# Pooling v in two halves of the heads, with three pairs of the first up matmul begun early

## The chip, the cores and the metric

The kernel runs on one core of a Trainium2 chip. The metric is the device time of one execution in microseconds (us); the time of a kernel is the median over its runs. The engines are called as in the profile: PE is TensorE (PEld its weight loads), DVE is VectorE, ACT is ScalarE, POOL is GpSimd, SP is SyncE. PSUM, into which PE writes, has eight banks of 512 fp32 values per partition. The kernel uses all of them: three pairs, called `banks[0]` to `banks[2]`, and two single ones, `obanks[0]` and `obanks[1]`.

## The reference

Attention over keys and values that are pooled by 8 along the sequence, and then a layer with the gate h * cos(h). Sizes: 8 batches, 8 heads, 576 positions, 64 values per head; the layer goes from 512 to 2048 and back, over 8 x 576 = 4608 tokens.

```python
def _attn_ref(q, k, v) -> np.ndarray:
    B, H, S, D = q.shape
    pool = 8
    Sp = S // pool
    scale = 1.0 / np.sqrt(D)
    k_p = k.reshape(B, H, Sp, pool, D).mean(axis=3)
    v_p = v.reshape(B, H, Sp, pool, D).mean(axis=3)
    scores = scale * np.matmul(q, k_p.transpose(0, 1, 3, 2))
    scores = scores - np.max(scores, axis=-1, keepdims=True)
    attn = np.exp(scores)
    attn = attn / (np.sum(attn, axis=-1, keepdims=True) + 1e-09)
    return np.matmul(attn, v_p).astype(np.float32)

def _moe_ref(x, w_in, w_out) -> np.ndarray:
    h = x @ w_in
    g = h * np.cos(h)
    return (g @ w_out).astype(np.float32)
```

Between the two, the attention's output is laid out as `x` with one row per token and 512 columns, head by head.

## The kernel before

The work runs over nine token tiles of 512 (`NT`, loop at L561). For tile t the kernel does an **up** stage (x times `w_in`, the gate) and a **down** stage (times `w_out`), and between these matmuls it puts the attention of batch t + 1, whose output fills the next tiles' x. x is held transposed in one SBUF tile, `xT`: 128 partitions by four chunks (`KCH`) by 4608 tokens. A chunk holds two heads, so chunks 0 and 1 are heads 0 to 3, and chunks 2 and 3 are heads 4 to 7.

The program's order on each engine is the order in which the code is written (`manual_schedule`, L53); what an instruction must wait for on other engines follows from the tiles that it reads and writes. So an instruction that waits holds up all that stands behind it on its engine.

Before tile 0, batch 0's attention runs alone (L533 to L556). Its first 512 positions are cut into four units, `BY_HEADS` (L50): units 0 and 1 are the positions 0 to 255 and 256 to 511 of heads 0 to 3, units 2 and 3 the same of heads 4 to 7. For each unit:

- `scores` (L222) multiplies pooled keys and transposed queries, and ACT takes the exponential (L240);
- `sums_first` (L306) sums the exponentials over the 72 pooled positions with a block of ones (four matmuls, L312), and ACT makes the inverse by a logarithm and an exponential (L316, L317);
- `values_then` (L320) multiplies the exponentials by the pooled values (four matmuls, L326), and DVE multiplies by the inverse and writes the unit's part of `xT` (L328).

`pool_v_mm` (L181) pools v: for each of 9 rows and each half of the partitions one matmul with the matrix `groups` (18 in all, L185), all heads at once, into both banks of a pair; then DVE copies the sums to `vz` (L187), from which `values_then` takes its weights. v is the last of batch 0's loads. While it travels, warm-up matmuls (L527), the pooling of k (L177), the transposes of q (L214), the scores and the first two units' sums run.

The tail of that stage is the part that the change touches. In order on PE: pooling of v into `banks[1]`; sums of unit 2 into `obanks[0]`; values of unit 0 into `obanks[1]`; values of unit 1 into `banks[1]`; sums of unit 3 into `banks[2]`; values of unit 2 into `obanks[1]`; values of unit 3 into `obanks[0]`. Then the first up matmuls begin.

An up stage has eight pairs of 128 hidden columns (`fp`, in tile 0 in the order 0 to 7). `up_mm` (L347) sums a pair's product over the four chunks into one pair of banks: four matmuls for chunks 0 and 1, four for chunks 2 and 3 (L353). In tile 0 the pairs take `banks[0]`, `banks[1]` and `banks[2]` in turn (L344). `up_g` (L357) takes the cosine on ACT (L363), for which the sine's table must be loaded (`sin_tables`, L333), and then the product on DVE (L367), which frees the banks for the third pair after. In tile 0 the chunks 0 and 1 of pairs 0 and 1 are multiplied before the loop (L557, L558), since they need only heads 0 to 3; the loop then does their chunks 2 and 3 (L568), and all four chunks of the later pairs. The weights `w_in` come in four blocks (`load_w_in`, L510 and L514), one for two pairs each.

Loads that change fp32 to bf16 are issued by POOL in the order of the code: for batch 0 q, k, q, v, then three blocks of `w_in`, then k and q of batch 1, the last block of `w_in`, and so on (L487 to L522).

Of the kernel before, what the change touches and what calls it, by code (L numbers as in the profile page):

```python
# [20 lines left out]
def kernel(  # L21
# [9 lines left out]
    nc = tc.nc  # L31
    B, H, S, D = q.shape
    Sp = S // POOL
# [4 lines left out]
    KCH = d_model // 128  # L38
# [45 lines left out]
    banks = [psum.tile([128, 2, 512], FP32, name=f"bank{i}") for i in range(3)]  # L84
    obanks = [psum.tile([128, 512], FP32, name=f"obank{i}") for i in range(2)]
# [51 lines left out]
    def v_part(b):  # L137
        return vz[b % 2][:, :, 0:4:3, :]
# [31 lines left out]
    def pool_k_mm(b, bank, pj0, pj1):  # L170

        kb = staged["k", b]
        ps = bank[:, 0:(pj1 - pj0) * Sp].rearrange("p (j n) -> p j n", n=Sp)
        for pj in range(pj0, pj1):
            for t in range(ROW):
                for rows in half:
                    nc.tensor.matmul(ps[rows, pj - pj0, :], lhsT=kb[rows, pj, t, :], rhs=groups[rows, t, :],  # L177
                                     start=(t == 0), stop=(t == ROW - 1))
        return lambda copy: put_kk(b, ps, pj0, pj1, copy)

    def pool_v_mm(b, pair):  # L181
        vb = staged["v", b]
        for t in range(ROW):
            for hp, rows in enumerate(half):
                nc.tensor.matmul(pair[:Sp, hp, 0:KCH * D], lhsT=groups[rows, t, :], rhs=vb[rows, :, t, :],  # L185
                                 start=(t == 0), stop=(t == ROW - 1))
        nc.vector.tensor_copy(out=v_part(b).rearrange("p j a d -> p a j d"),  # L187
                              in_=pair[:Sp, :, 0:KCH * D].rearrange("p a (j d) -> p a j d", j=KCH))

    def k_transpose(b):  # L190
        for i in range(2):
            nc.sync.dma_start_transpose(out=kk[b % 2][:, i * H // 2:(i + 1) * H // 2],
                                        in_=ring[b % 2][:, i:i + H].rearrange("p h d -> p (h d)"))
# [10 lines left out]
    def q_transpose(b):  # L204
        qT_tile(b)
        nc.sync.dma_start_transpose(out=att["qT", b], in_=q_flat(b))

    def q_transpose_mm(b, bank, g0, g1):

        if ("qT", b) not in att:  # L210
            qT_tile(b)
        ps = bank.bitcast(BF16)[:, 0:(g1 - g0) * 128].rearrange("p (g n) -> p g n", n=128)
        for g in range(g0, g1):
            nc.tensor.matmul(ps[:, g - g0, :], q_flat(b)[:, g * 128:(g + 1) * 128], identity, is_transpose=True)  # L214
        return lambda copy: copy(out=att["qT", b][:, g0:g1, :], in_=ps)

    def ex_col(u, i):

        (c0, n), (h0, nh) = u
        return (i // 2 % 2 * (nh // 2) + i // 4 * 2 + i % 2) * n  # L220

    def scores(b, u, pair):  # L222
        scores_mm(b, u, pair)
        scores_exp(b, u, pair)
# [19 lines left out]
    def x_out(b, u, rows):  # L244
        (c0, n), (h0, nh) = u
        return xT[rows, h0 // 2:(h0 + nh) // 2, b * S + c0:b * S + c0 + n]

    def cols(x, u):
        n = u[0][1]
        return x[:, 0:n * u[1][1] // 2].rearrange("p (j n) -> p j n", n=n)  # L250
# [3 lines left out]
    def inverse_tile(w):  # L254

        if early_inverses:
            name = early_inverses.pop(0)
            return msb.tile([128, 2, 256], FP32, name=name, tag=name, bufs=1).rearrange("p a m -> p (a m)")[:, 0:w]
        inv = asb.tile([128, 512], FP32, name="inv", tag="inv", bufs=1)
        return inv[:, 0:w]  # L260
# [45 lines left out]
    def sums_first(b, u, cs):  # L306

        (c0, n), (h0, nh) = u
        ex = att["ex", b, u]
        for i in range(nh):  # L310
            hp = i % 2
            nc.tensor.matmul(cs[hp * 64:hp * 64 + 64, (i // 2) * n:(i // 2 + 1) * n], lhsT=ones[:Sp, :],  # L312
                             rhs=ex[:, ex_col(u, i):ex_col(u, i) + n])
        w = nh * n // 2
        inv = inverse_tile(w)
        nc.scalar.activation(out=inv, in_=cs[:, 0:w], func=ACTF.Ln)  # L316
        nc.scalar.activation(out=inv, in_=inv, func=ACTF.Exp, scale=-1.0)  # L317
        att["inv", b, u] = inv

    def values_then(b, u, ao):  # L320

        (c0, n), (h0, nh) = u
        ex = att.pop(("ex", b, u))
        for i in range(nh):
            pj, hp = divmod(h0 + i, 2)
            nc.tensor.matmul(ao[hp * 64:hp * 64 + 64, (i // 2) * n:(i // 2 + 1) * n],  # L326
                             lhsT=vz[b % 2][:, pj, 3 * hp, :], rhs=ex[:, ex_col(u, i):ex_col(u, i) + n])
        nc.vector.tensor_mul(out=x_out(b, u, slice(0, 128)), in0=cols(ao, u), in1=cols(att.pop(("inv", b, u)), u))  # L328
# [4 lines left out]
    def sin_tables():  # L333
        nc.scalar.preload_act_table_set("trig_and_small")


    def up_order(t):
        n = FFCH // 2
        return range(n) if t < FIRST else [i + a * n // 2 for i in range(n // 2) for a in range(2)]

    def up_bank(t, fp):
        i = list(up_order(t)).index(fp)
        if t < FIRST:
            return banks[i % 3]  # L344
        return (banks[0], banks[2], banks[1], obanks)[i % 4 if i < 7 else 0]

    def up_mm(t, fp, k0=0, k1=KCH):  # L347

        h = up_bank(t, fp)
        for j in range(2):  # L350
            fc = 2 * fp + j
            for ki in range(k0, k1):
                nc.tensor.matmul(h[j] if h is obanks else h[:, j, :], lhsT=w_in_sb[fc // 4][:, ki, (fc % 4) * 128:(fc % 4 + 1) * 128],  # L353
                                 rhs=xT[:, ki, t * TILE:(t + 1) * TILE],
                                 start=(ki == 0), stop=(ki == KCH - 1))

    def up_g(t, fp, between=()):  # L357
        h = up_bank(t, fp)
        cos = msb.tile([128, 2, TILE], FP32, name="cos", tag="cos", bufs=2)
        g = g_sb[:, 2 * fp:2 * fp + 2, :]  # L360
        parts = [(h[j], cos[:, j], g[:, j]) for j in range(2)] if h is obanks else [(h, cos, g)]
        for ps, c, _ in parts:
            nc.scalar.activation(out=c, in_=ps, func=ACTF.Sin, bias=half_pi[:, :1])  # L363
        for put, copy in between:
            put(copy)
        for ps, c, o in parts:
            nc.vector.tensor_mul(out=o, in0=ps, in1=c)  # L367
# [31 lines left out]
    def put_gs(*kis):  # L399
        for k, i in kis:  # L400
            put_g(k, i)
# [93 lines left out]
    groups = g3.rearrange("p f n -> p (f n)")[:, 0:ROW * Sp].rearrange("p (t n) -> p t n", t=ROW)  # L495
# [34 lines left out]
    us = BY_HEADS  # L530
# [16 lines left out]
    warm_up(2, banks[1][:, 0, :])  # L547
    scores(0, us[2], banks[0])
    scores(0, us[3], banks[2])
    pool_v_mm(0, banks[1])  # L550
    sums_first(0, us[2], obanks[0])
    values_then(0, us[0], obanks[1])
    values_then(0, us[1], banks[1][:, 0, :])
    sums_first(0, us[3], banks[2][:, 0, :])
    values_then(0, us[2], obanks[1])
    values_then(0, us[3], obanks[0])  # L556
    up_mm(0, 0, 0, 2)  # L557
    up_mm(0, 1, 0, 2)  # L558
    sin_tables()

    for t in range(NT):  # L561
        b = t + 1
# [2 lines left out]
            for fp in up_order(t)[0:2]:  # L565
                up_mm(t, fp, 0, 2)
        for n, fp in enumerate(up_order(t)):
            up_mm(t, fp, 2 if n < 2 else 0)  # L568
            between = ()
            if t == 0:  # L570
                if fp == 4:
                    puts = pool_k_mm(1, obanks[0], 0, 2), pool_k_mm(1, obanks[1], 2, 4)
                elif fp in (5, 6):
                    g0 = 9 * (fp - 5)
                    puts = q_transpose_mm(1, obanks[0], g0, g0 + 5), q_transpose_mm(1, obanks[1], g0 + 5, g0 + 9)
                if fp in (4, 5, 6):
                    puts[0](vec)
                    between = ((puts[1], act),)
            up_g(t, fp, between)
            if 0 < t and 3 <= n < 6:  # L580
                put_gs(*[(k, 0) for k in (((3,), (1,), ()) if t == 1 else ((1, 2), (3,), (4,)))[n - 3]])
            if 0 < t and b < B:
                if n == 0:
                    q_transpose(b)
                    k_transpose(b)
                elif n == 2:
                    pool_rest(b, "v")
                    if b + 1 < B:
                        nc.gpsimd.tensor_copy(out=gate, in_=kk[b % 2][0:1, H - 1, 0:1])
                        load_q(b + 1)  # L590
                        load_kv(b + 1, "v", v)
            if n == 2:
                while stores:
                    stores.pop(0)()
# [155 lines left out]
```

The softmax here doesn't subtract the row's maximum and nothing guards it: scores larger than these inputs give would overflow.

## Time and profile before

| | |
|---|---|
| time, median of 4 runs | 286.49 us (286.07 to 287.55) |
| the profiled execution, its own time | 287.55 us |
| its span, first to last instruction | 285.8 us |
| granted PE clock, mean | 1.00 |
| stretch 13.16 to 18.34 us: PE, DVE, ACT busy | 3.58, 2.02, 4.49 us of 5.18 |
| stretch 18.34 to 36.50 us: PE, DVE, ACT busy | 18.16, 12.55, 13.38 us of 18.16 |
| DMA in both stretches | 206 and 207 GB/s |

The stretches are cut where the work changes: from 13.16 the last scores of batch 0 and the tail just described, from 18.34 the up stage of tile 0 with the pooling of batch 1's k and the transposes of its q between. Times in the trace count from the first instruction. An engine's busy time is what its rows add up to; a matmul's row lasts from its start until its last result is written, so that rows of matmuls that follow each other overlap, and the pace is read from their starts. An idle time is put down to the semaphore that ended it.

### The profile page before, as it was taken

The page shows a single profiled execution, that of the slowest core. Times are in us where ns is not written, and L with a number is a line of the kernel's source. Part 1 is how long each engine was busy: PE and PEld are TensorE (multiplying, and loading weights), DVE is VectorE, ACT ScalarE, POOL GpSimd, SP SyncE. Part 2 cuts the span into 40 slices and gives each one's busy share as a digit, 9 for nine tenths or more (in the row PEclk, how much of TensorE's full clock was granted, in tenths as well). Part 3 has the DMA queues.
Part 4 walks back from the last instruction along what each step waited for, and adds up shares of the span by engine and source line. Part 5 has one row for each costly group of instructions (what it writes and reads, how often), then busy time and mean ns, then how long its engine had stood idle before and what let it go on. Part 6 is the DMA issues. An engine that isn't in the chain of part 4 may idle for free.

```text
span 285.8 us, 5857 instructions
## 1 busy us (share of the span) xinstructions
PE 277.0 (97%) x2360; PEld 176.8 (62%) x2360; DVE 215.3 (75%) x314; ACT 164.4 (58%) x193; POOL 143.0 (50%) x150
## 2 busy tenths in 40 slices
PE   7889999999999999999999999999999999999994
PEld 3445554445874597458845884588448844874583
DVE  5547747899966995699569956995699569856972
ACT  3677798377356745665566556565556555436600
POOL 8453159997499349934993399439900000000000
PEclk9999999999999999999999999999999999999999
DMA  7999999592929798998677968892670252005014
GB/s 148 200 205 206 207 205 214 104 213 37 166 40 150 128 226 137 144 145 182 101 141 144 183 94 159 137 189 55 115 158 3 55 117 50 0 20 129 2 37 110
DMA packets 57738, 36.12 MB, mean 126 GB/s; under 512 B 35441, under 2 KB 53361, under 8 KB 57713
## 3 DMA queue, kind: packets, MB, share of 16 engines
q0 software_dynamic: 19744, 18.07, 41.3%
q1 hardware_dynamic: 37328, 17.18, 29.3%
q10 hardware_dynamic: 640, 0.52, 0.8%
q8 instruction: 18, 0.29, 0.4%
q14 instruction: 8, 0.06, 0.1%
HBM read 36.70 MB, written 9.44 MB: 161 GB/s over the span
## 4 chain that ended last, share of the span: by engine, by line
PE 86%; DVE 6%; ACT 3%; DMA 2%; issue 1%; POOL 0%; DVEq 0%; POOLq 0%; ACTq 0%
PE bank L353 35%; PE obank L431 32%; PE obank L370 4%; PE obank L353 4%; PE bank L233 3%; DVE g_sb L367 3%; DMA q_b<-in_q_dram 2%; PE bank L295 2%; PE bank L431 2%; PE bank L268 1%; DVE w L387 1%; DVE g L397 1%; ACT cos L363 1%; ACT ex L240 1%; DVE vz L187 0%
## 5 line engine op out<-in xcount | busy, mean ns | idle before, releaser
L353 PE MATMUL bank<-xT,w_in_sb 128*128 128x512 bf16 x512 | 114.0, 379 | 0.2 <-DVE g_sb L367 0.2
L363 ACT ACTIVATE cos<-bank,half_pi 128x1024 f32<-128x1024 f32 x64 | 70.3, 1113 | 57.0 <-PE bank L353 55.1
L353 PEld LDWEIGHTS <-w_in_sb 128*128 128x128 bf16 x576 | 56.1, 98 | 66.3 <-issue 0.9
L367 DVE TENSOR_TENSOR g_sb<-bank,cos 128x1024 bf16<-128x1024 f32 x64 | 77.1, 1218 | 25.1 <-ACT cos L363 24.8
L156 POOL TENSOR_TENSOR half_sums<-kv_st 72x512 f32<-72x512 bf16 x48 | 54.8, 1168 | 0.6 <-issue 0.2
L240 ACT ACTIVATE ex<-bank 72x1024 bf16<-72x1024 f32 (+1 forms) x40 | 35.0, 928 | 34.0 <-PE bank L233 33.8
L431 PEld LDWEIGHTS <-g 128*128 128x128 bf16 x512 | 47.9, 98 | 6.1 <-issue 0.3
L431 PE MATMUL obank<-w,g 128*128 128x256 bf16 x368 | 42.7, 272 | 0.2 <-DVE p_sb L445 0.2
L431 PEld LDWEIGHTS <-g_sb 128*128 128x128 bf16 x384 | 36.7, 98 | 6.9 <-DVE g_sb L367 0.3
L162 POOL TENSOR_TENSOR half_sums<-half_sums 72x512 f32<-72x512 f32 x24 | 30.4, 1289 | 0.0
L431 PE MATMUL obank<-w_out_sb,g_sb 128*128 128x256 bf16 x240 | 28.9, 273 | 0.0
L397 DVE TENSOR_TENSOR g<-g_sb 128x1024 bf16<-128x1024 bf16 x32 | 23.3, 729 | 0.5
L714 POOL COPY gate<-g 1x1 bf16<-1x1 bf16 x5 | 0.9, 180 | 34.5 <-DVE g L397 34.5
L279 DVE TENSOR_TENSOR xT<-bank,inv 64x256 bf16<-64x256 f32 x14 | 5.9, 422 | 15.0 <-ACT inv L275 14.9
L300 DVE TENSOR_TENSOR x_rows<-bank,inv_rows 128x512 bf16<-128x512 f32 x24 | 16.6, 691 | 0.8
L431 PE MATMUL obank<-w_out_sb,g 128*128 128x256 bf16 x112 | 15.6, 273 | 0.0
L431 PE MATMUL obank<-w,g_sb 128*128 128x256 bf16 x128 | 15.3, 273 | 0.0
L370 PE MATMUL obank<-w_out_sb,g_sb 128*128 128x512 bf16 x64 | 15.2, 379 | 0.0
L353 PE MATMUL obank<-xT,w_in_sb 128*128 128x512 bf16 x64 | 15.1, 379 | 0.0
L233 PE MATMUL bank<-qT,kk 64*72 64x128 bf16 (+2 forms) x288 | 12.7, 221 | 0.1
L233 PEld LDWEIGHTS <-kk 64*72 64x72 bf16 x288 | 8.8, 110 | 5.3 <-issue 3.8
L331 ACT ACT_TABLE_LOAD x9 | 11.5, 1283 | 0.9 <-PEq L734 0.8
(103 smaller groups left out, 277.6 us busy)
## 6 DMA issues: line engine op xcount, KB each, us to landing
out_dram<-o_two SPq DMA_DIRECT2D x64, 128.0 KB, 2.4
kv_st<-in_v_dram POOLq DMA_DIRECT2D x8, 576.0 KB, 11.4
kv_st<-in_k_dram POOLq DMA_DIRECT2D x7, 576.0 KB, 8.2
q_b<-in_q_dram POOLq DMA_DIRECT2D x6, 576.0 KB, 7.5
w_in_sb<-in_moe_w_in_dram POOLq DMA_DIRECT2D x4, 512.0 KB, 14.5
w_out_sb<-in_moe_w_out_dram POOLq DMA_DIRECT2D x4, 512.0 KB, 18.2
q_b<-in_q_dram POOLq DMA_DIRECT2D x4, 288.0 KB, 13.2
g_sb<-in_k_dram SPq DMA_DIRECT2D x1, 576.0 KB, 3.5
```

The source lines that it names most:

```text
L156: nc.gpsimd.tensor_tensor(out=s[:, h:h + 2], in0=x[:, h:h + 2, 0:4, :], in1=x[:, h:h + 2, 4:8, :], op=ADD)
L162: add(out=s[:, h:h + 4, 0:2, :], in0=s[:, h:h + 4, 0:2, :], in1=s[:, h:h + 4, 2:4, :], op=ADD)
L233: nc.tensor.matmul(pair[:Sp, bank, c:c + n].rearrange("p (g n) -> p g n", n=64), lhsT=kk[b % 2][half[r], key_slot(b, h0 + i, r), 0:Sp], rh ...
L240: nc.scalar.activation(out=ex[:, 0:nh * n].rearrange("p (a n) -> p a n", a=2), in_=pair[:Sp, :, 0:nh * n // 2], func=ACTF.Exp, scale=scale ...
L300: nc.vector.tensor_tensor(out=x[0:n].rearrange("p (j a d) -> p j a d", j=KCH, a=2), in0=ps[0:n, :, 0:2 * (D + 2)].rearrange("p j (a w) -> ...
L331: nc.scalar.preload_act_table_set("natural_log_exp_and_others")
L353: nc.tensor.matmul(h[j] if h is obanks else h[:, j, :], lhsT=w_in_sb[fc // 4][:, ki, (fc % 4) * 128:(fc % 4 + 1) * 128], rhs=xT[:, ki, t * ...
L363: nc.scalar.activation(out=c, in_=ps, func=ACTF.Sin, bias=half_pi[:, :1])
L367: nc.vector.tensor_mul(out=o, in0=ps, in1=c)
L370: nc.tensor.matmul(o, lhsT=g_sb[:, fc, ms * 128:(ms + 1) * 128], rhs=w_out_sb[fc // 4][:, fc % 4, :], start=(fc == 0), stop=(fc == FFCH - 1))
L397: nc.vector.tensor_tensor(out=out[:, f0:f1], in0=x, in1=y, op=op)
L431: mms.append(lambda bank=bank, first=first, g=g, w=w, fc=fc, p=p: nc.tensor.matmul(bank[p], lhsT=g(fc, p), rhs=w(fc), start=(first and fc ...
```

## The change

`pool_v_mm` takes a range of chunks, and pools and copies these alone; without a range it does all four, as it does for batch 1. For batch 0 it is called twice: chunks 0 and 1 (heads 0 to 3), and chunks 2 and 3 after the values of unit 0. The 18 matmuls on 256 columns become twice 18 on 128 columns, the copy of 512 values per partition becomes two of 256. Both halves write to the first columns of `banks[1]`.

The order of the tail becomes: first half of v; values of unit 0 (`obanks[1]`); second half of v; values of unit 1 (now `obanks[0]`); sums of unit 2 (now `banks[0]`); values of unit 2 (`obanks[1]`); sums of unit 3 (`banks[2]`); values of unit 3 (`obanks[0]`). Chunks 0 and 1 of three pairs, not two, are then multiplied before the loop, and the loop leaves them out for three pairs in tile 0.

```diff
-    def pool_v_mm(b, pair):
+    def pool_v_mm(b, pair, j0=0, j1=KCH):
         vb = staged["v", b]
         for t in range(ROW):
             for hp, rows in enumerate(half):
-                nc.tensor.matmul(pair[:Sp, hp, 0:KCH * D], lhsT=groups[rows, t, :], rhs=vb[rows, :, t, :],
+                nc.tensor.matmul(pair[:Sp, hp, 0:(j1 - j0) * D], lhsT=groups[rows, t, :], rhs=vb[rows, j0:j1, t, :],
                                  start=(t == 0), stop=(t == ROW - 1))
-        nc.vector.tensor_copy(out=v_part(b).rearrange("p j a d -> p a j d"),
-                              in_=pair[:Sp, :, 0:KCH * D].rearrange("p a (j d) -> p a j d", j=KCH))
+        nc.vector.tensor_copy(out=v_part(b)[:, j0:j1].rearrange("p j a d -> p a j d"),
+                              in_=pair[:Sp, :, 0:(j1 - j0) * D].rearrange("p a (j d) -> p a j d", d=D))
...
     scores(0, us[3], banks[2])
-    pool_v_mm(0, banks[1])
-    sums_first(0, us[2], obanks[0])
+    pool_v_mm(0, banks[1], 0, 2)
     values_then(0, us[0], obanks[1])
-    values_then(0, us[1], banks[1][:, 0, :])
+    pool_v_mm(0, banks[1], 2, 4)
+    values_then(0, us[1], obanks[0])
+    sums_first(0, us[2], banks[0][:, 0, :])
+    values_then(0, us[2], obanks[1])
     sums_first(0, us[3], banks[2][:, 0, :])
-    values_then(0, us[2], obanks[1])
     values_then(0, us[3], obanks[0])
-    up_mm(0, 0, 0, 2)
-    up_mm(0, 1, 0, 2)
+    for fp in range(3):
+        up_mm(0, fp, 0, 2)
     sin_tables()
...
         for n, fp in enumerate(up_order(t)):
-            up_mm(t, fp, 2 if n < 2 else 0)
+            up_mm(t, fp, 2 if n < (3 if t == 0 else 2) else 0)
```

## The prediction

> **What bounds the kernel now.** I read the page's busy times first, then the chain that ended last, in order of time, then the timeline of the stretch that the change touches.
>
> ```profile
> span 285.8 us, 5857 instructions
> PE 277.0 (97%) x2360; PEld 176.8 (62%) x2360; DVE 215.3 (75%) x314; ACT 164.4 (58%) x193; POOL 143.0 (50%) x150
> ...
> 15.74 0.70 DVE vz L187
> ...
> 18.37 8.80 PE bank L353 x40
> 27.17 1.29 PE obank L177 x72
> 28.46 1.83 PE bank L353 x8
> ```
>
> TensorE is the bound. It is idle 8.8 us in all; the table by stretch puts 1.6 us of that into 13.16 to 18.34, the tail of batch 0's attention, and none into 18.34 to 36.5. From 18.34 the chain is TensorE without a break, so what moves the first up matmul, or opens a gap in the up stage, is paid in full. Now the timeline (start, duration, engine, line, count, idle before and its releaser):
>
> ```profile
> 14.47 1.17 PE L185 MATMUL bank<-kv_st,g 64*72 64x256 bf16 x18 [0.69 <-DMA kv_st<-in_v_dram]
> 15.57 0.41 PE L312 MATMUL obank<-ex,ones 72*64 72x256 bf16 x4
> 15.74 0.69 DVE L187 CAST vz<-bank 72x512 bf16<-72x512 f32 x1 [2.66 <-ACT ex L240]
> 16.03 0.60 ACT L316 ACTIVATE q_sb<-obank 128x512 f32<-128x512 f32 x1
> 16.48 0.41 PE L326 MATMUL obank<-ex,vz 72*64 72x256 bf16 x4 [0.50 <-DVE vz L187]
> 16.72 0.39 PE L326 MATMUL bank<-ex,vz 72*64 72x256 bf16 x4
> 16.94 0.39 PE L312 MATMUL bank<-ex,ones 72*64 72x256 bf16 x4
> 17.00 0.69 DVE L328 TENSOR_TENSOR xT<-obank,p_sb 128x512 bf16<-128x512 f32 x1 [0.58 <-PE obank L326]
> 17.75 0.63 PE L326 MATMUL obank<-ex,vz 72*64 72x256 bf16 x8 [0.42 <-DVE xT L328]
> 18.34 8.83 PE L353 MATMUL bank<-xT,w_in_sb 128*128 128x512 bf16 x40
> 19.06 1.28 ACT L334 ACT_TABLE_LOAD   x1
> 21.13 1.11 ACT L363 ACTIVATE cos<-bank,half_pi 128x1024 f32<-128x1024 f32 x1 [0.79 <-PE bank L353]
> 22.28 1.23 DVE L367 TENSOR_TENSOR g_sb<-bank,cos 128x1024 bf16<-128x1024 f32 x1 [2.51 <-ACT cos L363]
> ```
>
> v lands at 14.47, and nothing before that moves. The pooling, its copy and the products follow in turn, with two waits of 0.50 and 0.42.
>
> The rows from 18.34 on decide my forecast. The 40 up matmuls follow each other by (8.83 - 0.38)/39 = 0.217 us. Pair 0 (half of it begun early, then pair 1's half, then its rest) is whole after 12 matmuls, 18.34 + 2.60 = 20.94; its cosine starts 0.19 later and its product ends at 22.28 + 1.23 = 23.51. Pair 3 reuses bank 0 and has its turn after 24 matmuls, at 18.34 + 5.20 = 23.54. **The bank comes free 0.03 us before it is wanted: there is no slack.**
>
> **The change part by part.** Lags, all from these rows: TensorE to VectorE 0.10, TensorE to ScalarE 0.05, VectorE to TensorE 0.05, ScalarE to VectorE 0.04. VectorE rows follow each other 0.08 before the nominal end (17.00, then 17.61), ScalarE's Ln and Exp by 0.63. Four products take 0.41, the next group of the same tile shape starts 0.23 after them, one of another shape 0.07 before their end (15.57 against 15.64).
>
> *Half the pooling.* The 256-column matmuls follow by (1.17 - 0.27)/17 = 0.053 us. The Trainium skill (TensorE: Matmul & The Clock Gate, "Wait — 56ns, not 53.3ns?") gives columns / 2.4 GHz + 2.5 ns one after another: 109 ns for 256 columns, 56 for 128. The row shows half of that, since the two row halves of the array work side by side, so I take 0.027 for 128 columns. By the row a half takes 17 x 0.027 + 0.21 (a 128-column transposing matmul's own time, from L214: five in 0.45 at 0.056) = 0.67; by the rule 1.16. I take the row and keep the other end: L177's 72 matmuls in 1.36, each with its own weights, show that loading does not hold them at 0.05.
>
> *Half the copy.* 256 elements: 0.42 (L279 with 256 elements a partition took 422 ns, L328 with 512 took 691, L187 with 512 took 686). Two halves cost 0.84 for 0.69.
>
> *The switches of shape.* The Trainium skill (TensorEngine Tiling (Array Packing), "Key Properties") says that changing the tiling mode drains TensorE, which speaks against putting the second half between two groups of products: two switches more. The row prices one: the next group starts 0.07 before the last end, so some 0.15 of overlap is lost at each (0.2 after the last issue where 0.05 is usual). By the row that is 0.3 of TensorE's time; with no drain 0. I count it, though waits cover most of it.
>
> In order, then (us of the span):
> - half 1 14.47 to 15.14; copy 1 15.24 to 15.66; values of unit 0 15.71 to 16.12 (before: 16.48, so 0.77 earlier);
> - half 2 16.05 to 16.72; values of unit 1 16.65 to 17.06; sums of unit 2 16.88 to 17.29;
> - VectorE: product of unit 0 16.22 to 16.91, copy 2 16.83 to 17.25, product of unit 1 17.17 to 17.86;
> - values of unit 2 wait for copy 2: 17.30 to 17.71; sums of unit 3 17.53 to 17.94; values of unit 3 need obank 0, which the product of unit 1 reads until 17.86: 17.91 to 18.32. Behind this wait on TensorE stands only the up stage;
> - up begins at 18.28: **0.06 gained of the 0.77**. The wait that is late next is VectorE: copy 2 and the two products fill it from 16.22 to 17.86.
> - ScalarE gets the sums of unit 2 at 17.34 instead of 16.03: Ln, Exp, Ln, Exp from 17.34, 17.97, 18.59, 19.21 to 19.84. The product of unit 3 runs 19.88 to 20.57 (before 19.77), the sine table ends at 21.14 (before 20.34). Cover: 12 early matmuls, 18.28 + 2.60 = 20.88, instead of 8. Without the third pair the rest of pair 0 would start at 18.28 + 1.73 = 20.01 and wait 0.6. So the third pair does hide that.
>
> *What the third pair costs.* No matmul is added, but four now stand ahead of the rest of pair 0. It is whole after 16: 18.28 + 3.47 = 21.75; cosine 21.94, product 1.15 later at 23.09, ended 24.32. Pair 3 has its turn at 18.28 + 5.20 = 23.48 and waits for bank 0 until 24.37: **a new stall of 0.89**. Against 23.54 before, pair 3 is 0.83 late. Afterwards cosines and products follow without another wait: pair 1's product ends 25.44, wanted at 26.10; pair 2's 26.6, wanted at 27.8.
>
> *Transfers.* No DMA is added or passed. One is wanted earlier: pair 2's first half uses the second block of w_in at 18.28 + 8 x 0.217 = 20.01 instead of 21.8. Loads issued on POOL wait for the landing of the one eight before (v of batch 1 until 17.23 for w_in block 0, w_out until 22.30 for block 2); the issue between, which would wait for block 1, goes at 19.89 with no wait shown. So it has landed by then, with 0.1 to 0.4 to spare; were it late, 0.2 at most.
>
> **Sum.** -0.06 + 0.89 = +0.83 us, from TensorE's own continuous chain. What follows doesn't take it back: up to 36.5 TensorE has no idle time, 0.3 us in 36.5 to 50; the piece of the chain on VectorE at 54.39 starts on TensorE's last down matmul, and after 66.68 TensorE has no wait of note. The profiled execution took 287.55 us, 1.75 around its span, and was the slowest of the four; 288.4 against it, and **287.3** against the median of 286.49: +0.29%.
>
> **Rivals.**
> (a) *Halves that don't run at half the time* (56 ns a matmul). Half 1 ends 15.63, values of unit 0 start 16.20, half 2 ends 17.70, copy 2 18.22, product of unit 1 18.83, values of unit 3 18.88, up 19.25; pair 3 at 19.25 + 6.09 = 25.34: +1.80, **288.3**, slower by 0.6%. For it: the rule. Against it: L177 and L185. It decides once up starts 0.54 later than now, at 18.88: 0.54 + 0.89 = 1.43, half a per cent.
> (b) *The second copy holds unit 1's values*, if the order between copy and product is kept by whole tile: values of unit 1 at 17.30, product of unit 1 ends 18.50, up 18.92, pair 3 25.01: +1.47, **288.0**. Against it: up begins at 18.34 before the products of units 2 and 3 have written their part of the same xT tile (19.08 and later), so parts are told apart.
> (c) *No net loss*: the gap is made up later or up starts earlier. Break-even needs up at 23.54 - 6.09 = 17.45, but the values of unit 2 start only at 17.30 and eight matmuls and a shared bank follow. Made up later: **286.4**. For it only the chain's stretch on VectorE; against it that it starts from TensorE.
> (d) *The clock*: the first ten matmuls take 0.43 each, later ones 0.217. If the gaps brought the slow clock back for 3 to 4 us, half of that is lost: +1.7 more, **289**. Against it: gaps of 0.7 now don't do that, and the new ones are 0.6 and 0.9.
>
> **How the numbers follow.** About 0.5%, 1.4 us, is what a measurement of this kernel can tell from no change. Forecast (+0.4 to +1.2) 0.74; (a) 0.07; (b) 0.04; (d) 0.03; (c) 0.08, of which 0.03 is faster by over 0.5%; something unseen of the slower kind 0.04. So faster 0.03, same 0.79, slower 0.18. The range: 286.4 from (c) to 288.7, just beyond (a).
>
> **What would show it.** Right: a gap of some 0.9 before the seventh group of up matmuls (the 25th), put down to VectorE's product at L367; up starting at 18.2 to 18.3; the first cosine at 21.9; both halves of L185 at about 0.67. Wrong: up before 17.5; no gap at pair 3; a half of over 1 us; the values of unit 1 behind the second copy; a wait for w_in before pair 2.

## The result, and the profile after

The changed kernel takes 287.54 us (median of 32 runs, 286.64 to 290.31) against 286.44 us (53 runs, 285.67 to 287.79): ratio 1.0035, 95% interval 1.0026 to 1.0045, so 0.7 to 1.3 us more, 1.0 in the middle. The forecast was 287.3 us, 0.83 more.

The profiled execution of the changed kernel took 287.19 us and has a span of 285.4 us, shorter than the 285.8 us of the one before. That isn't the change: here v landed 1.2 us earlier, ahead of everything that the change touches. So the two timelines are read from the first pooling matmul of v, not from the start of the span. The timeline after (start, duration, engine, line, count, idle before and its releaser):

```profile
13.28 0.69 PE L185 MATMUL bank<-kv_st,g 64*72 64x128 bf16 x18 [0.26 <-DMA kv_st<-in_v_dram]
14.54 0.41 PE L326 MATMUL obank<-ex,vz 72*64 72x256 bf16 x4 [0.57 <-DVE vz L187]
14.88 0.69 PE L185 MATMUL bank<-kv_st,g 64*72 64x128 bf16 x18
15.50 0.41 PE L326 MATMUL obank<-ex,vz 72*64 72x256 bf16 x4
15.67 0.41 DVE L187 CAST vz<-bank 72x256 bf16<-72x256 f32 x1
16.17 0.60 ACT L316 ACTIVATE q_sb<-bank 128x512 f32<-128x512 f32 x1 [0.87 <-PE bank L312]
16.77 0.41 PE L326 MATMUL obank<-ex,vz 72*64 72x256 bf16 x4
17.11 5.35 PE L353 MATMUL bank<-xT,w_in_sb 128*128 128x512 bf16 x24
18.61 0.69 DVE L328 TENSOR_TENSOR xT<-obank,p_sb 128x512 bf16<-128x512 f32 x1 [0.45 <-ACT p_sb L317]
20.77 2.12 ACT L363 ACTIVATE cos<-bank,half_pi 128x1024 f32<-128x1024 f32 x2 [0.90 <-PE bank L353]
21.92 3.69 DVE L367 TENSOR_TENSOR g_sb<-bank,cos 128x1024 bf16<-128x1024 f32 x3 [2.62 <-ACT cos L363]
23.20 3.61 PE L353 MATMUL bank<-xT,w_in_sb 128*128 128x512 bf16 x16 [0.74 <-DVE g_sb L367]
```

The run of 40 up matmuls is now two, 24 and 16, with a wait between them that ends with a product on VectorE. Taken from v:

| from the first pooling matmul of v, us | before | forecast | after |
|---|---|---|---|
| values of unit 0 begin | 2.01 | 1.24 | 1.26 |
| up begins | 3.87 | 3.81 | 3.83 |
| product of unit 3 ends | 5.30 | 6.10 | 6.02 |
| first cosine | 6.66 | 7.47 | 7.49 |
| first matmul of pair 3 | 9.07 | 9.90 | 9.92 |

The last row, called **the distance** below, is 0.85 us longer. TensorE's list of waits names the stall as well. Its line for the up matmuls' wait on the product at L367, first before, then after (engine, line, what it waited for: us in total, times, longest):

```profile
PE bank L353 <- DVE g_sb L367: 0.2, 1, 0.2
PE bank L353 <- DVE g_sb L367: 0.9, 2, 0.7
```

The one wait before lies later, behind 36 us. The start of pair 3 before, 23.54, is counted by pace. The matmuls' own rows put it slightly later:

```profile
23.09 0.84 PE L353 MATMUL bank<-xT,w_in_sb 128*128 128x512 bf16 x3
```

The third of these is pair 3's first, and a matmul takes 0.38, so it starts at 23.09 + 0.84 - 0.38 = 23.55, not at 23.09 + 2 x 0.217 = 23.52. By the rows the distance before is thus 9.08, and 0.84 longer after. In the experiments below, too, starts counted by pace come out up to 0.03 early where no stall stands at pair 3.

From pair 3's first matmul to the end of the span it is 285.8 - 23.54 = 262.3 us before and 285.4 - 23.20 = 262.2 us after. Nothing later gives the loss back or adds to it.

### The profile page after: what moved, and what is told of

The parts are those of the page before. It is cut to its first block, busy times and chain, and to the rows that moved or that the text cites. A ratio compares the mean times of both kernels' runs of the same rounds, so it can differ in the third digit from the quotient of the medians.

```text
span 285.4 us, 5893 instructions
## 1 busy us (share of the span) xinstructions
PE 276.6 (97%) x2378; PEld 176.4 (62%) x2378; DVE 215.4 (75%) x315; ACT 164.2 (58%) x193; POOL 143.5 (50%) x150
## 4 chain that ended last, share of the span: by engine, by line
PE 86%; DVE 7%; ACT 3%; DMA 2%; issue 1%; POOL 0%; POOLq 0%; DVEq 0%; ACTq 0%
PE bank L353 35%; PE obank L431 32%; PE obank L370 4%; PE obank L353 4%; PE bank L233 3%; DVE g_sb L367 3%; DMA q_b<-in_q_dram 2%; PE bank L295 2%; PE bank L431 2%; ACT cos L363 2%; PE bank L268 1%; DVE w L387 1%; DVE g L397 1%; ACT ex L240 1%; PE bank L185 1%
## 5 line engine op out<-in xcount | busy, mean ns | idle before, releaser
L367 DVE TENSOR_TENSOR g_sb<-bank,cos 128x1024 bf16<-128x1024 f32 x64 | 77.1, 1219 | 25.2 <-ACT cos L363 24.9
```

## The experiments

My theory: the loss is the wait for bank 0 that the third early pair makes, and the late inverses are a second cost that the third pair hides. The main rivals: the loss comes from the late sums alone, or from the splitting itself (drains, the second copy). Each kernel is judged by its distance and by its time.

**The changed kernel with two early pairs.**

```diff
-    for fp in range(3):
+    for fp in range(2):
...
-            up_mm(t, fp, 2 if n < (3 if t == 0 else 2) else 0)
+            up_mm(t, fp, 2 if n < 2 else 0)
```

> The changed kernel with two early pairs as before. Measure: the distance from the first pooling matmul of v to the first matmul of pair 3 (9.07 us before, 9.92 after). My theory, two causes: the late sums hold the rest of pair 0 until the product of unit 3 is done (6.0 after v), so pair 0 is whole later too: distance 9.5 to 9.6, about +0.5 us, ratio 1.0017, with a wait of some 0.6 before the rest of pair 0 and next to none at pair 3. Rival (the third pair is the whole cost): distance 9.0, ratio 0.9998.

Its timeline:

```profile
12.85 0.69 PE L185 MATMUL bank<-kv_st,g 64*72 64x128 bf16 x18 [0.33 <-DMA kv_st<-in_v_dram]
16.69 1.90 PE L353 MATMUL bank<-xT,w_in_sb 128*128 128x512 bf16 x7
18.19 0.69 DVE L328 TENSOR_TENSOR xT<-obank,p_sb 128x512 bf16<-128x512 f32 x1 [0.46 <-ACT p_sb L317]
18.93 7.10 PE L353 MATMUL bank<-xT,w_in_sb 128*128 128x512 bf16 x32 [0.35 <-DVE xT L328]
```

The rest of pair 0 starts when the product of unit 3 has ended, 6.08 after v, and the 32 matmuls from there run without a gap that the list shows (the trace lacks one record of the eight ahead); pair 3 is the 17th of them, at 18.93 + 16 x 0.217 = 22.40: distance 9.55, as the theory has it. The time: 286.63 us, ratio 1.0008 (0.9996 to 1.0020), which leaves both open, so it was measured again:

> The changed kernel with two early pairs once more: its first measurement, 1.0008 with an interval from 0.9996 to 1.0020, holds both the 0.5 us of my theory (1.0017) and the rival's nothing (0.9998). Theory: 1.0010 to 1.0020 with the distance 9.55 again. Rival: 0.9995 to 1.0005.

Ratio 1.0004 (0.9994 to 1.0014), distance 19.84 + 3.47 - 13.77 = 9.54. By time this expectation failed: 0.5 us would be 1.0017. The trace has the wait both times, and from pair 3 to the end it is 262.2 and 262.3 us as in the others, so the 0.5 us is in these two executions. But both ratios lie nearer to the rival's value than to mine, the median of the kernel before was itself 286.38, 286.47 and 286.72 in the three sets of runs, and v's first matmul lies anywhere from 12.74 to 14.47 in the profiled executions. The cost of the late inverses alone is shown by the traces and not by the times.

**The kernel before with a third early pair**, and nothing else.

```diff
-    up_mm(0, 0, 0, 2)
-    up_mm(0, 1, 0, 2)
+    for fp in range(3):
+        up_mm(0, fp, 0, 2)
...
-            up_mm(t, fp, 2 if n < 2 else 0)
+            up_mm(t, fp, 2 if n < (3 if t == 0 else 2) else 0)
```

> The kernel before with nothing changed but a third early pair. My theory: four matmuls more ahead of the rest of pair 0, a wait of 0.7 to 0.9 at pair 3 for bank 0, distance 9.95, +0.89 us, ratio 1.0031. Rival (it costs only together with the late sums, or is free by itself): distance 9.1, ratio 1.0000.

Ratio 1.0027 (1.0017 to 1.0037). Its timeline:

```profile
12.85 1.17 PE L185 MATMUL bank<-kv_st,g 64*72 64x256 bf16 x18 [0.32 <-DMA kv_st<-in_v_dram]
16.72 5.34 PE L353 MATMUL bank<-xT,w_in_sb 128*128 128x512 bf16 x23
17.45 0.69 DVE L328 TENSOR_TENSOR xT<-obank,p_sb 128x512 bf16<-128x512 f32 x1
22.79 3.61 PE L353 MATMUL bank<-xT,w_in_sb 128*128 128x512 bf16 x16 [0.73 <-DVE g_sb L367]
```

The same wait, 0.73 beside 0.74, and the distance 9.94. (The count of 23 is a matmul record that the trace lacks.) The third pair alone gives the loss. It hides nothing here: the product of unit 3 ends 18.14, and the rest of pair 0 with two early pairs would start at 16.72 + 1.73 = 18.45.

**The sums of unit 2 early**, with two early pairs and with three. The tail, in both:

```diff
     pool_v_mm(0, banks[1], 0, 2)
+    sums_first(0, us[2], banks[0][:, 0, :])
     values_then(0, us[0], obanks[1])
     pool_v_mm(0, banks[1], 2, 4)
     values_then(0, us[1], obanks[0])
-    sums_first(0, us[2], banks[0][:, 0, :])
     values_then(0, us[2], obanks[1])
```

> The changed kernel with the sums of unit 2 put right behind the first half of v (while its copy runs), and two early pairs. My theory: the inverses are early enough again, the rest of pair 0 finds its x ready, no stall at pair 3: distance 9.0 to 9.2, ratio 0.9995 to 1.0005. Rival (splitting the pooling costs by itself, by drains and the extra copy): distance 9.4 or more, ratio 1.001 or more.

> The changed kernel with the sums of unit 2 put right behind the first half of v, three early pairs. My theory: the third pair costs the same whether the inverses are early or late: distance 9.9, ratio 1.003. Rival (the late sums are the cause and the third pair only shows it): distance 9.1, ratio 1.000.

With three pairs:

```profile
12.74 0.69 PE L185 MATMUL bank<-kv_st,g 64*72 64x128 bf16 x18 [0.43 <-DMA kv_st<-in_v_dram]
22.66 3.61 PE L353 MATMUL bank<-xT,w_in_sb 128*128 128x512 bf16 x16 [0.74 <-DVE g_sb L367]
```

Ratio 1.0040 (1.0026 to 1.0054), distance 22.66 - 12.74 = 9.92, with the same wait of 0.74. Two pairs: ratio 1.0010 (0.9990 to 1.0029), but the profiled execution has TensorE at half its clock at the start of up. In the table of one-microsecond stretches for TensorE (stretch, its length, busy time and count, granted clock, DMA share, GB/s):

```profile
16.00:17.00 1.00, 0.78 (x16) 1.00 1.23 205
17.00:18.00 1.00, 0.99 (x13) 0.86 1.25 208
18.00:19.00 1.00, 0.78 (x3) 0.50 1.22 204
19.00:20.00 1.00, 1.00 (x4) 0.50 1.24 207
20.00:21.00 1.00, 1.00 (x4) 0.50 1.23 210
21.00:22.00 1.00, 1.00 (x6) 0.94 1.22 209
```

In a stretch at half the clock 3 and 4 matmuls are counted, and 6 at the full one (one that reaches over an edge counts on both sides, and the stretch with 3 lacks a record). Of its 14 runs four lie at 288.2 to 288.6 with a mean clock of 0.994, the other ten at 286.0 to 286.9. So it was run again, beside a version with the wait filled:

> The early-sums kernel with two early pairs once more, beside the filled one, for the share of executions with a spell of half clock and for a profile without one. Theory: where there is no spell, the distance from the first pooling matmul of v to pair 3 is 9.0 to 9.2 and the time that of the kernel before, 286.2 to 286.6; with one, about 1.8 us more. Rival (the split pooling costs by itself): distance 9.4 or more without a spell.

Without a spell now:

```profile
13.66 0.69 PE L185 MATMUL bank<-kv_st,g 64*72 64x128 bf16 x18 [0.52 <-DMA kv_st<-in_v_dram]
17.49 8.84 PE L353 MATMUL bank<-xT,w_in_sb 128*128 128x512 bf16 x40
```

Forty matmuls in one run again, distance 17.49 + 5.20 - 13.66 = 9.03, ratio 1.0007 (0.9991 to 1.0022). So, as far as 0.05 us of distance and 0.2% of time can tell, **splitting v costs nothing by itself and gains nothing**, apart from the spells of half clock: with the inverses in time and two early pairs the distance is that of the kernel before, and the third pair puts some 0.9 us on top of it.

```diff
     pool_v_mm(0, banks[1], 0, 2)
+    warm_up(2, obanks[0])
     sums_first(0, us[2], banks[0][:, 0, :])
```

> The kernel with early sums and two early pairs, and two warm-up matmuls more, which fill TensorE's wait between the first half of v and the sums of unit 2. They compute nothing that is used. Theory: the spells of half clock that some executions of the early-sums kernel show at the start of up come from TensorE's idle time in the tail; with the wait filled none of some 14 executions is above 288, and the ratio is 0.9995 to 1.0010 (the two matmuls may push the rest by 0.1 to 0.2). Rival (the spells come whatever TensorE does): again a quarter of them above 288.

Ratio 0.9991 (0.9971 to 1.0011), 14 runs from 286.05 to 287.46, none with a mean clock under 0.997; its distance is 17.70 + 5.20 - 13.76 = 9.14. More on this at the end.

**A version meant to beat both**: the halves straight behind each other, and the units' values and sums in banks that, as I thought, no product still reads; two early pairs. The tail, and the second half's copies, one for each of its two banks (its matmuls write to `obanks[hp]`):

```diff
     pool_v_mm(0, banks[1], 0, 2)
-    values_then(0, us[0], obanks[1])
-    pool_v_mm(0, banks[1], 2, 4)
-    values_then(0, us[1], obanks[0])
+    pool_v_mm(0, obanks, 2, 4)
+    values_then(0, us[0], banks[1][:, 0, :])
+    values_then(0, us[1], banks[1][:, 1, :])
     sums_first(0, us[2], banks[0][:, 0, :])
-    values_then(0, us[2], obanks[1])
     sums_first(0, us[3], banks[2][:, 0, :])
-    values_then(0, us[3], obanks[0])
+    values_then(0, us[2], obanks[0])
+    values_then(0, us[3], obanks[1])
...
+        if pair is obanks:
+            for hp in range(2):
+                nc.vector.tensor_copy(out=vz[b % 2][:, j0:j1, 3 * hp, :],
+                                      in_=pair[hp][:Sp, 0:(j1 - j0) * D].rearrange("p (j d) -> p j d", d=D))
```

> A version meant to beat both: v still in two halves, but the second half straight behind the first (into the two single banks, with two copies of 128 values each), then the values of units 0 and 1, both sums, the values of units 2 and 3 in banks that no product still reads; two early pairs. My theory: the tail waits no longer for a shared bank or for the second copy, up starts 3.1 us after the first pooling matmul of v instead of 3.87; where v comes early the exponentials of units 2 and 3 hold the inverses, and the rest of pair 0 then waits up to 0.6. Distance to pair 3 8.3 to 8.9, gain 0.15 to 0.75 us, ratio 0.9975 to 0.9995. Rival (the products on VectorE and the inverses on ScalarE bound the tail whatever the order of TensorE): distance 9.0 or more, ratio 1.000 or more.

Ratio 1.0026 (1.0018 to 1.0035): slower, and the theory's number missed. The timeline shows why:

```profile
14.29 0.41 PE L331 MATMUL bank<-ex,vz 72*64 72x256 bf16 x4
14.74 0.69 DVE L333 TENSOR_TENSOR xT<-bank,p_sb 128x512 bf16<-128x512 f32 x1
15.49 0.41 PE L331 MATMUL bank<-ex,vz 72*64 72x256 bf16 x4 [0.79 <-DVE xT L333]
16.15 0.60 ACT L321 ACTIVATE q_sb<-bank 128x512 f32<-128x512 f32 x1 [1.30 <-PE bank L317]
19.33 7.10 PE L358 MATMUL bank<-xT,w_in_sb 128*128 128x512 bf16 x32 [0.60 <-DVE xT L333]
```

The values of unit 1 go to the second bank of a pair whose first bank the product of unit 0 reads, and they wait 0.79 us until that product is done (14.74 + 0.69 = 15.43). The sums stand behind them, ScalarE sits idle 1.30 us, and the rest of pair 0 waits 0.60 for the product of unit 3: distance 19.33 + 3.47 - 13.03 = 9.77, which is the 0.7 us of the time. The rival named the right engines, but what held them was the pair.

The same order and banks with v pooled whole, as an edit to the kernel before:

```diff
     pool_v_mm(0, banks[1])
-    sums_first(0, us[2], obanks[0])
-    values_then(0, us[0], obanks[1])
-    values_then(0, us[1], banks[1][:, 0, :])
+    values_then(0, us[0], banks[1][:, 0, :])
+    values_then(0, us[1], banks[1][:, 1, :])
+    sums_first(0, us[2], banks[0][:, 0, :])
     sums_first(0, us[3], banks[2][:, 0, :])
-    values_then(0, us[2], obanks[1])
-    values_then(0, us[3], obanks[0])
+    values_then(0, us[2], obanks[0])
+    values_then(0, us[3], obanks[1])
```

> The same order and banks, but v pooled whole as before, so that only the halves are taken away; two early pairs. My theory: the values of unit 0 start as late as before, 2.0 after v, and the gain is gone: distance 9.0 to 9.1, ratio 0.9995 to 1.0005. Rival (the banks and the order give the gain, the halves nothing): distance 8.3 to 8.9, ratio below 0.9995.

Ratio 1.0095 (1.0066 to 1.0125). Neither expectation fits. Here the values of unit 0 themselves wait 0.83 for the copy, and those of unit 1 wait 0.86 for the product of unit 0:

```profile
16.98 0.41 PE L326 MATMUL bank<-ex,vz 72*64 72x256 bf16 x4 [0.86 <-DVE xT L328]
```

The sums come so late that the product of unit 3 ends 20.09 + 0.69 - 13.71 = 7.07 after v, 1.8 later than before. Its profiled execution has a spell of half clock too. Of its six runs four have a mean clock of 0.988 or 0.994; the other two took 288.1 and 288.3 us, 1.7 and 1.9 above the kernel before, of which the late product accounts for some 1.5 (the rest of pair 0 can start 7.1 after v, in place of 5.6). The run says nothing on what the halves are worth; beside the version above it only shows that they let the tail start earlier. I didn't go on with this order: even without the shared pair, ScalarE has two exponentials (1.9 us) and four rows of inverses (2.5 us) to do from about v's arrival on, and the product of unit 3 behind them, so, as an estimate from these rows, the rest of pair 0 could start 5.2 after v instead of 5.6 where the exponentials begin as v arrives. That was not tried. No version ran that beats the kernel before clear of its noise.

## Why the prediction was right

**The base.** TensorE's chain from up on is paid in full: right. The stretch from pair 3 to the end is 262.2 to 262.3 us in both kernels and in all of the experiments whose pair 3 could be timed.

**Half the pooling.** The row of two array halves side by side, 0.67, against 1.16 for one matmul after another: measured 0.69. Rival (a) is out.

**Half the copy and the switches of shape.** 0.42 and 0.41 for the two copies; each group behind a switch starts 0.07 before the end of the last, as priced. The early-sums kernel with two pairs, distance 9.03, shows that the split copy and the switches together do not lengthen the way to pair 3.

**0.06 of 0.77 gained.** Measured 0.04 (3.83 against 3.87): the values of unit 0 are 0.75 earlier, and the copy and two products on VectorE take it back.

**The late inverses, hidden by the third pair.** Right by the trace: without the third pair the rest of pair 0 waits (0.35 in the row, 0.5 counted from its turn) for the product of unit 3. The forecast had 0.6, since it put that product's end 0.08 too late.

**The stall of 0.89.** From its turn, 17.11 + 24 x 0.217 = 22.31, to 23.20: 0.89. The row has 0.74, since it counts from the end of the last matmul. One small step was off: by the forecast's own lag from VectorE to TensorE, 0.05, a bank that comes free at 23.51 can't be used before 23.56, so the "slack" of 0.03 was already a wait of 0.02 to 0.03 in the kernel before.

**The second block of w_in** was there in time: TensorE's list of waits after has none for it.

**Rival (b)**, the second copy holding unit 1's values, is out as it was put: they begin at 15.50, before that copy at 15.67. But its kind of order by whole tile does exist, between the two banks of one pair. **Rival (c)** is out with the constant 262.2. **Rival (d)**, the clock, did not come in the profiled execution of the changed kernel, whose table has 1.00 throughout the stretch. It came in two kernels of the study, for 3.4 us and at the price of 1.7 us that was put on it. The reason given against it, that gaps of 0.7 don't bring it on, is no safe one: one spell came behind a longest wait of 0.51.

The forecast of 0.83 lies inside the measured 0.7 to 1.3. The profiles show 0.84 or 0.85; what the middle of the interval has beyond it I leave open, since v's landing moves single executions by more than that.

## What to carry to other kernels

Before work is begun early, ask what the producer ahead of it completes, and who waits for that: four matmuls put ahead of a bank's last four delay its release by their whole length, and where the release was just in time (0.03 us here), that is the price. A copy that is split makes the first consumer earlier, but look at the engine that both halves and the consumers' own products share; here VectorE took back 0.7 of 0.75 us. Where a load's landing moves from execution to execution, read two traces from that landing, not from the start.

## What I had not expected of the hardware and the program's order

**Half the clock without a long gap.** In the table of the early-sums kernel above the granted clock is at half from about 17.7 to 21.1 us. That costs 0.14 + 3 x 0.50 + 0.06 = 1.7 us, although TensorE's longest wait in the four microseconds ahead of it was 0.51. The profiled execution with v pooled whole and other banks has a spell of the same length, 18.5 to 21.9, behind waits of 0.83 and 0.86.

Of the other runs only the mean clock is known; one such spell makes it 0.994. A mean of 0.993 or 0.994 was seen, with early sums, in 4 of 14 and 2 of 13 runs with two pairs and in 3 of 21 with three, and in none of 14 with two warm-up matmuls in the wait. If the share were that of the unfilled ones (9 of 48), 14 runs without any would come about one time in twenty. So the filling may be the reason, but that is not shown, and the length of one wait doesn't decide it: the version with the halves in a row waited 0.79 and had no such run in 21. Single runs with a lower mean clock still (0.982 or 0.988) came in the kernel before and in the changed one too; where in them the clock fell is not known. What brings a spell on stays open.

**Two banks of one pair are not always apart.** A matmul to the second bank waited for a product that read only the first (0.79 and 0.86 us). Parts of one tile in SBUF did not hold each other up in the same stretch of the changed kernel: the values of unit 1 read `vz` at 15.50, before the second copy writes its part of it from 15.67, and up reads `xT` from 17.11, before the product at 18.61 writes its part.

**v's landing.** The first pooling matmul of v began between 12.74 and 14.47 in the profiled executions of kernels whose programs are the same up to there.
